# A planned attention and feed-forward kernel: other durations for GpSimd and SP, and a delay before GpSimd may take a high part

## The chip, the cores and the metric

The kernel runs on one core of a Trainium2 chip. The core has five engines that run side by side, each through its own list of instructions in a fixed order: TensorE (PE, matrix products), VectorE (DVE), ScalarE (ACT), GpSimd (POOL) and SyncE (SP), which here only issues transfers (DMA). An instruction waits until the instructions on other engines whose results it needs have signalled. The metric is the device time of one execution in microseconds (us); a smaller time is better.

## The reference

Two stages, the output of the first being the input of the second. Inputs are float32: q, k, v of 8 batches, 8 heads, 576 positions, 64 columns; f of 8 x 8 x 576; w_in of 512 x 2048 and w_out of 2048 x 512.

```python
scores = scale * np.matmul(q, k.transpose(0, 1, 3, 2))
log_f = np.log(np.clip(f, 0.0001, 1.0))
cum = np.cumsum(log_f, axis=-1)
decay = cum[:, :, :, None] - cum[:, :, None, :]
scores = np.where(causal, -1000000000.0, scores + decay)
scores = scores - np.max(scores, axis=-1, keepdims=True)
attn = np.exp(scores)
attn = attn / (np.sum(attn, axis=-1, keepdims=True) + 1e-09)
attn_out = np.matmul(attn, v)
...
x = attn_out.transpose(0, 2, 1, 3).reshape(4608, 512)
h = x @ w_in
g = np.where(h >= 1, h, np.where(h <= -1, 0.0, (h + 1) ** 2 / 4))
return g @ w_out
```

So: causal attention with a decay that depends on the distance of two running sums, and then for each of 4608 tokens a feed-forward layer with a piecewise quadratic activation between two products.

## The kernel before

**Split numbers.** Most products run on float16 pairs: a float32 value, scaled by a power of two, is written as a high part (the value rounded to float16) and a low part (value minus high part, again float16). A product of two such values takes three products of halves. The high part is a multiplication by a scale, which ScalarE, VectorE or GpSimd can do (helper `times`, L395 to L401: ScalarE at L397, GpSimd at L401); the low part is a two-input instruction on VectorE, and it waits for the high part.

**Attention** (`attention`, L687 on) runs in 36 jobs, one for two heads of one batch, with batch 0 cut in two (`CUTS`). A job loads q and k (L717, L721) and the running sums, spread over all partitions (tile ck, L730), all issued by SP. From job 12 on, ScalarE finds the largest magnitudes (L780), a small exchange through TensorE spreads them (`across`, L440 on), GpSimd makes the factors (`factors`, L795), q and k are split (tile qs; high parts by `X`, low parts at L818 and L824), and SP issues one DMA transpose of the 20 blocks (L833) and two copies that swap halves (tile qkT, L837). The first jobs work in float32 through TensorE transposes (L756, L767, L1021).

For each of the five row tiles r of 128 queries (the last has 64 for each head, both heads in one tile), GpSimd makes the decay into a tile sd or sdr: a multiply-add over (r + 1) x 128 columns (L934), then a select that puts a very small number above the diagonal (L938). TensorE makes the scores into one of three banks (tile s; L846). VectorE adds both and takes the row minimum (its sign is turned; L971), which also empties the bank; ScalarE takes the exponential and its row sum (L980); GpSimd or VectorE adds the small constant (`inverse`, L986), VectorE takes the reciprocal (L992). Then the weights are scaled and split into tile pr: the high part on ScalarE or GpSimd (by `X`), the low part on VectorE (L1056). SP issues the DMA transpose of pr into pT (L1068; for the last row tile two, L1073). TensorE multiplies pT with the split v (tile vs, L896), and ScalarE and VectorE write the two halves of x (L912, L913).

**Feed-forward** (`moe`, L1098 on) runs over 18 chunks of 256 tokens, and for each over 8 blocks of 256 columns of w_in: 24 matmuls into ph (L1119); ScalarE makes the scaled rectified value (L1128) and its square (L1131), VectorE joins them into u (L1132, which empties ph), then come the high part of g (`X`; L397 or L401), the low part of g on VectorE (L1138), and 12 matmuls into po (L1146), 8 that need only the high part and 4 that need the low one. At the chunk's end po goes to ot and out to memory. The weights are loaded at the start in eight blocks and split there (`weight_split`): the high part on ScalarE, the low part (`low`) in two GpSimd instructions (L572, L573) or in one of VectorE.

**The order** is not written by hand. Every instruction group is registered by `Order.op` with its engine, an estimated duration, what it reads and writes, and a priority; an operation may name other engines with their durations (`other`) and, for each, a time `late` that must have passed since the operation became ready. `Order.plan` then plays the whole kernel through with these durations: whenever an engine is free it takes, in order of priority, the first operation that is ready and whose buffers are free. Engines are asked in the order of their first registered operation, and the first one registered is a memset on GpSimd. What is played through becomes the order in which each engine's instructions are written, and also settles which engine does an operation that several can do. At run time nothing is changed any more: an instruction whose inputs come later than planned holds up all that stands behind it on its engine.

The helpers give the durations: `act_us`, `dve_us`, `pool_us` by the number of columns; `V`, `A`, `G`, `M` register for VectorE, ScalarE, GpSimd and TensorE; `X` registers an operation with a choice of engines ("AG": ScalarE or GpSimd); `L` registers a transfer with the time SP needs to issue it and its size, `T` a DMA transpose with its number of blocks. After a GpSimd operation the plan lets GpSimd go on 0.04 us before its end (`OVER`). The plan lets a transfer land at the later of its issue's end plus a constant, and of the point at which the DMA engines have moved its bytes plus a constant. `hold` keeps job 9 and later from starting before a planned time, 27 us apart (`PACE`).

Of the kernel before, what the change touches and what calls it, by code (L numbers as in the profile page):

```python
# [37 lines left out]
WLOAD = (-98.0, -50.0, -40.0, -30.0, -6.0, 0.0, 6.0, 12.0)  # L38
SLACK = 0.3
WINDOW = 1000  # L40

# [30 lines left out]
class Order:  # L72
# [42 lines left out]
    def plan(self):  # L115
        ops = self.ops
        n = len(ops)
# [23 lines left out]
        while done < n:  # L141
# [5 lines left out]
            while again:  # L147
                again = False
                for eng, l in waiting.items():
# [57 lines left out]
                    if size:  # L207
                        kind = "DMA"
                        begin = max(t, dma - 4.0)
                        free[eng] = begin + dur  # L210
                        dma = max(dma, begin + 0.3) + size
                        end = max(begin + dur + 1.7, dma + 1.4)
                    else:
                        begin = t
                        if eng == "PE" and md != mode:
                            begin += 0.1
                            mode = md
                        end = begin + dur
                        free[eng] = end - self.OVER[eng]
# [41 lines left out]
def pool_us(n):  # L261
    return 0.36 + 0.001 * n

# [6 lines left out]
def kernel(  # L270
# [149 lines left out]
    def T(blocks, emit, reads=(), writes=(), prio=0.0):  # L420
        op("SP", 0.95 + 0.055 * blocks + (2.3 if blocks > 20 else 0.0), emit, reads, writes, prio, blocks * 0.0328 * 6.0)

# [17 lines left out]
    def across(m, n, mkeys, prio):  # L440
# [16 lines left out]

        op("POOL", 0.55, make, ["ident"], [top, dg], prio, other=[("DVE", 0.4, 0.0)])
        M(
# [18 lines left out]
    def decay_sums():  # L478
# [3 lines left out]
        pr = -99.0  # L482
        L(0.5, 0.15, lambda: nc.sync.dma_start(fl[0:nb, 0:S], f.rearrange("b h s -> (b h) s")), [], key, pr)
        V(S, lambda: nc.vector.tensor_scalar(
# [7 lines left out]
        ), ["flz"], key, pr, 1.35)  # L492
        L(0.5, 0.15, lambda: nc.sync.dma_start(cum_d, cum), key, ["cum_d"], pr)
        pt = Buf(f_pool)
# [17 lines left out]
    def weight_load(i, prio):  # L512
# [4 lines left out]
        for j in range(2):  # L517
            src, raw = srcs[j], raws[RAW[i][j]]
            n = src.shape[1] // 2
            for part in range(2):  # L520
                dst = raw[:, 2 * DM * part:2 * DM * (part + 1)].rearrange("p (t c) -> p t c", t=n)
                L(
                    0.45, 0.524, lambda dst=dst, src=src, part=part, n=n: nc.sync.dma_start(
                        dst, src[:, n * part:n * part + n, :]
                    ), [], [rawkeys[RAW[i][j]][part]], prio + 0.1 * j + 0.05 * part,
                )

    def weight_split(i, prio):
# [29 lines left out]
        for j in range(2):  # L558
# [15 lines left out]

            op("POOL", 3.5, low, [("sw", i)], key + [("pl", i, j)], prio, other=[("DVE", 1.46, 0.0)])

    def load_values(b, hp, prio):
        s_ = v[b, 2 * hp:2 * hp + 2]
        t = vres[hp]
        for hh in range(2):  # L580
            L(0.45, 0.131, lambda hh=hh: nc.sync.dma_start(
                t[:, hh, 0:LAST, :], s_[hh, 0:FULL, :].rearrange("(t p) d -> p t d", p=P)
            ), [], [("v", hp, hh)], prio)
        L(0.45, 0.033, lambda: nc.sync.dma_start(
            t[0:64, :, LAST, :], s_[:, FULL:S, :].rearrange("h p d -> p h d")
# [56 lines left out]
    def moe_scales(b, k, first, last, prio):  # L642
# [37 lines left out]

        G(1.2, make, [("sv", b), ("rv", b), ("lim", k)] + need, [z.key], prio)
        return z
# [4 lines left out]
    def attention(ji):  # L687
# [11 lines left out]
        for j, src in enumerate((q, k)):  # L699
# [16 lines left out]
            for hh in range(2):  # L716
                L(0.45, 0.131, lambda part=part, s_=s_, hh=hh, full=full, t0=t0: nc.sync.dma_start(  # L717
                    part()[1][:, hh, 0:full - t0, :], s_[hh, P * t0:P * full, :].rearrange("(t p) d -> p t d", p=P)
                ), [], [keys[hh]], pr - 20)
            if r1 == NT5:  # L720
                L(0.45, 0.033, lambda part=part, s_=s_, nt=nt: nc.sync.dma_start(  # L721
                    part()[1][0:64, :, nt - 1, :], s_[:, FULL:S, :].rearrange("h p d -> p h d")
# [4 lines left out]
        for h in range(2):  # L727
            ck = Buf(ck_first if p < NPE else ck_pool)
            cks.append(ck)
            L(0.5, 0.29, lambda ck=ck, h=h: nc.sync.dma_start(  # L730
                ck.ap[:, 0:s1], cum_d[bh + h:bh + h + 1, 0:s1].broadcast_to([P, s1])
# [39 lines left out]
        else:  # L771
# [24 lines left out]

            G(0.9, factors, [mk, sc, "cq"], [sg, cs], pq)
            nsig, nalpha = (lambda: sg.ap[:, 0:1]), (lambda: sg.ap[:, 1:2])
# [37 lines left out]
            for h in range(2):  # L836
                L(0.5, 0.3, lambda h=h: nc.sync.dma_start(  # L837
                    qt.ap[64 * h:64 * h + 64, n:n + nqe], qt.ap[64 - 64 * h:128 - 64 * h, 0:nqe]
# [80 lines left out]
        for r in range(r0, r1):  # L919
# [5 lines left out]
            for h in range(2):  # L925
# [16 lines left out]

                G(pool_us(wid) + 0.34, decay, [cks[h], "sdz"] + sigkey, [(sd, h if r == LAST else 0)], pw)

# [45 lines left out]

            op("POOL", 0.26, inverse, [(sm, i) for i in range(nh)], [rc], pw, other=[("DVE", 0.22, 0.0)])
            V(0, lambda rc=rc, nh=nh: nc.vector.reciprocal(rc.ap[:, 0:nh], rc.ap[:, 0:nh]), [], [rc], pw, 0.25)  # L992
            part = int(r >= 2)
# [46 lines left out]
            else:  # L1040
# [5 lines left out]
                for i, sd in enumerate(sds):  # L1046
# [3 lines left out]
                    def rows_(sd=sd, cols=cols):  # L1050
# [3 lines left out]
                        e, prv()[:, :, 0, i, :], rows_(), rc.ap[:, i:i + 1]  # L1054
                    ), kk + [rc], [(prb, i)], pw + 0.5)
                    V(cols, lambda i=i, prv=prv, rows_=rows_, rc=rc: nc.vector.scalar_tensor_tensor(  # L1056
# [41 lines left out]
    def moe(ch, first, last, z, prio):  # L1098
# [10 lines left out]
        for fb in range(first, last + 1):  # L1109
# [3 lines left out]
            for fi in range(2):  # L1113
# [22 lines left out]
                e, g.ap[:, 0], u.ap, z.r[:, i:i + 1]  # L1136
            ), [u, z.key], [(g, 0)], pf - 1e4)
            V(512, lambda i=i, u=u, g=g: nc.vector.scalar_tensor_tensor(  # L1138
# [101 lines left out]
```

## Time and profile before

| | |
|---|---|
| median of 3 runs | 1122.61 us |
| lowest, highest | 1117.22, 1122.67 us |
| the profiled execution | 1119.65 us |
| its span, first to last instruction | 1117.9 us |
| mean granted clock of TensorE | 0.985 |

Transfers of the page that belong to what SP issues (operation, count, size, median us from issue to landing):

```profile
ck<-cum_d SPq DMA_DIRECT2D x62, 288.0 KB, 3.9
...
qkT<-qkT SPq DMA_DIRECT2D x48, 160.0 KB, 3.5
```

In the profile, PE is TensorE's products and PEld its weight loads, DVE is VectorE, ACT ScalarE, POOL GpSimd, SP SyncE. A group's row names the line, the engine, the operation, what is written and read, its shape and count, then the total busy time in us and the mean of one in ns, then the idle time of the engine just before these instructions and who ended it. A row of the waits reads "who waited <- who ended the wait: us in total, how many, the longest". A row of busy time over a stretch gives for each engine the busy us and the number of instructions, then the granted clock of TensorE, the DMA engines' share and GB/s. The lines themselves stand in the prediction.

### The profile page before, as it was taken

How to read it: one execution, taken by the hardware profiler on the slowest of the kernel's cores; microseconds unless marked ns; L12 is line 12 of the kernel's file. 1: busy time of each engine (PE TensorE's matmuls, PEld its weight loads, DVE VectorE, ACT ScalarE, POOL GpSimd, SP SyncE). 2: the span in 40 equal slices, each digit the busy share in tenths (PEclk: the TensorE clock that was granted, in tenths of full speed). 3: DMA queues.
4: the chain of work that ended last, by engine and by line, in shares of the span. 5: the costliest groups of instructions: out<-in, count | busy, mean ns of one | idle time of the engine just before them, and what ended most of it. 6: DMA issues, size and time to landing. Idle time of an engine off the chain costs nothing. (4 is left out here: it accounts for less than half of the span.)

```text
span 1117.9 us, 24870 instructions
## 1 busy us (share of the span) xinstructions
PE 1047.2 (94%) x8805; PEld 696.7 (62%) x8805; DVE 815.0 (73%) x2033; ACT 651.2 (58%) x1396; POOL 673.5 (60%) x1153
## 2 busy tenths in 40 slices
PE   4878999899999999999999999999999999999998
PEld 2545655556755766666766665665766677677665
DVE  5878888887888978888887878887877864232332
ACT  3556766665766765676757675766657653232232
POOL 2578787776777766876776776776676741111110
PEclk9879999999999999999999999999999999999999
DMA  7845455776987878789878886887768662000000
GB/s 190 294 128 162 135 139 106 137 144 139 169 168 156 170 145 166 152 152 167 154 149 156 156 173 144 161 169 141 149 141 167 116 105 37 21 20 20 1 19 20
DMA packets 390620, 146.37 MB, mean 131 GB/s; under 512 B 367328, under 2 KB 368352, under 8 KB 390496
## 3 DMA queue, kind: packets, MB, share of 16 engines
q1 hardware_dynamic: 385312, 135.35, 60.0%
q10 hardware_dynamic: 5184, 9.44, 2.5%
q8 instruction: 69, 1.13, 0.4%
q14 instruction: 55, 0.45, 0.2%
HBM read 65.68 MB, written 9.58 MB: 67 GB/s over the span
## 5 line engine op out<-in xcount | busy, mean ns | idle before, releaser
L1146 PE MATMUL po<-place,g 128*128 128x512 f16 x1728 | 405.4, 381 | 10.9 <-POOL g L401 8.2
L1119 PE MATMUL ph<-x,place 128*128 128x256 f16 (+3 forms) x4608 | 407.0, 247 | 3.0 <-DVE u L1132 1.5
L1119 PEld LDWEIGHTS <-place 128*128 128x128 f16 x4608 | 355.7, 98 | 57.2 <-issue 7.4
L1146 PEld LDWEIGHTS <-g 128*128 128x128 f16 x1728 | 162.5, 98 | 199.1 <-POOL g L401 14.3
L1128 ACT ACTIVATE u<-ph,z 128x512 f32<-128x512 f32 x144 | 110.9, 771 | 173.1 <-PE ph L1119 153.3
L401 POOL TENSOR_SCALAR g<-u,z 128x512 f16<-128x512 f32 x94 | 74.4, 791 | 218.7 <-DVE u L1132 203.7
L1132 DVE SCALAR_TENSOR_TENSOR u<-ph,z,u 128x512 f32<-128x512 f32 x144 | 107.4, 747 | 122.9 <-ACT u L1131 121.9
L980 ACT ACTIVATE sdr<-sdr,nm 128x512 f32<-128x512 f32 (+3 forms) x246 | 135.9, 553 | 82.3 <-DVE nm L971 75.0
L934 POOL TENSOR_SCALAR sdr<-ck,sg,cqs 128x128 f32<-128x128 f32 (+1 forms) x192 | 157.5, 820 | 34.2 <-DVE pr L1056 26.7
L1138 DVE SCALAR_TENSOR_TENSOR g<-u,z,g 128x512 f16<-128x512 f32 x144 | 113.6, 790 | 57.4 <-POOL g L401 48.3
L1056 DVE SCALAR_TENSOR_TENSOR pr<-sdr,nm,pr 128x128 f16<-128x128 f32 (+1 forms) x224 | 130.6, 614 | 5.9 <-POOL pr L401 3.1
L971 DVE CUSTOM_DVE_ANT_0 sdr<-s,sdr,sg 128x128 f32<-128x128 f32 (+1 forms) x192 | 100.9, 542 | 15.3 <-PE s L846 12.1
L938 POOL TENSOR_SCALAR_AFFINE_SELECT sdr<-sdr 128x128 f32<-128x128 f32 x246 | 95.9, 390 | 18.1
L846 PE MATMUL s<-qkT 128*128 128x128 f16 (+5 forms) x576 | 94.6, 297 | 9.8 <-DVE nm L971 7.0
L397 ACT ACTIVATE pr<-sdr,nm 128x256 f16<-128x256 f32 (+3 forms) x133 | 70.2, 549 | 48.9 <-issue 18.5
L1131 ACT ACTIVATE u<-u 128x512 f32<-128x512 f32 x144 | 90.6, 630 | 4.5
L896 PE MATMUL s<-pT,vs 128*64 128x320 f16 (+4 forms) x1176 | 68.9, 263 | 5.8 <-DVE nm L971 2.5
L896 PEld LDWEIGHTS <-vs 128*64 128x64 f16 x1176 | 56.5, 110 | 28.2 <-issue 19.2
L401 POOL TENSOR_SCALAR pr<-sdr,nm 128x512 f16<-128x512 f32 (+3 forms) x91 | 54.5, 601 | 17.3 <-DVE nm L992 12.9
L846 PEld LDWEIGHTS <-qkT 128*128 128x128 f16 (+1 forms) x576 | 41.5, 101 | 37.2 <-issue 19.9
L934 POOL TENSOR_SCALAR sd<-ck,sg,cqs 64x576 f32<-64x576 f32 x48 | 42.3, 881 | 20.6 <-DVE pr L1056 18.5
L767 PE MATMUL s<-qkT 64*128 64x128 f32 (+5 forms) x192 | 49.2, 513 | 5.4 <-DVE nm L971 4.3
(147 smaller groups left out, 1215.9 us busy)
## 6 DMA issues: line engine op xcount, KB each, us to landing
ck<-cum_d SPq DMA_DIRECT2D x62, 288.0 KB, 3.9
out_dram<-ot ACTq DMA_DIRECT2D x36, 256.0 KB, 3.0
v<-in_v_dram SPq DMA_DIRECT2D x64, 128.0 KB, 3.3
qk<-in_k_dram SPq DMA_DIRECT2D x64, 128.0 KB, 2.7
qkT<-qkT SPq DMA_DIRECT2D x48, 160.0 KB, 3.5
qk<-in_q_dram SPq DMA_DIRECT2D x56, 128.0 KB, 3.2
place<-in_moe_w_in_dram SPq DMA_DIRECT2D x10, 512.0 KB, 6.2
place<-in_moe_w_out_dram SPq DMA_DIRECT2D x8, 512.0 KB, 8.5
```

The costliest lines, as they stand in the source:

```text
L401: nc.gpsimd.tensor_scalar(out=out, in0=in_, scalar1=scale, scalar2=0.0, op0=ALU.mult, op1=ALU.add)
L846: nc.tensor.matmul(sp[p0:p1, 0:c1 - c0], lhsT=tq[:, h, q0 - s0:q0 - s0 + p1 - p0], rhs=tk[:, h, c0:c1], start=(c == 0), stop=(c == 1),)
L896: nc.tensor.matmul(av.ap[64 * h:64 * h + 64, c0:n], lhsT=vs.ap[:, vl, h, t, :], rhs=pT.ap[:, t, pl, h, c0:n], start=(t == 0 and pi == 0), ...
L934: nc.gpsimd.tensor_scalar(out=sd.ap[p0:p1, 0:wid], in0=cks[h].ap[p0:p1, 0:wid], scalar1=ns if p < NQK else ns[p0:p1], scalar2=cqs()[p0:p1, ...
L971: V(0, lambda o=i + ci, sd=sd, sp=sp[ci], c0=c0, c1=c1, nm=nm: nc.vector.tensor_tensor_reduce(out=sd.ap[:, c0:c1], in0=sp.ap[:, 0:c1 - c0] ...
L980: A(wid, lambda i=i, sd=sd, wid=wid, nm=nm, sm=sm: nc.scalar.activation(sd.ap[:, 0:wid], sd.ap[:, 0:wid], AF.Exp, bias=nm.ap[:, i:i + 1], ...
L1056: V(cols, lambda i=i, prv=prv, rows_=rows_, rc=rc: nc.vector.scalar_tensor_tensor(out=prv()[:, :, 1, i, :], in0=rows_(), scalar=rc.ap[:, i ...
L1119: nc.tensor.matmul(ph.ap[:, fi * TC + a0:fi * TC + a1], lhsT=wi[fb][:, wl, t, fi * P:(fi + 1) * P], rhs=xs[b][:, t, xl, s0:s0 + a1 - a0], ...
L1128: A(512, lambda i=i, ph=ph, u=u: nc.scalar.activation(u.ap, ph.ap, AF.Relu, scale=z.u[:, i:i + 1], bias=z.h[:, i:i + 1]), [ph, z.key], [u] ...
L1132: V(512, lambda i=i, ph=ph, u=u: nc.vector.scalar_tensor_tensor(out=u.ap, in0=ph.ap, scalar=z.t[:, i:i + 1], in1=u.ap, op0=ALU.max, op1=AL ...
L1138: V(512, lambda i=i, u=u, g=g: nc.vector.scalar_tensor_tensor(out=g.ap[:, 1], in0=u.ap, scalar=z.r[:, i:i + 1], in1=g.ap[:, 0], op0=ALU.mu ...
L1146: nc.tensor.matmul(po.ap[i], lhsT=g.ap[:, gl, fi * TC + i * P:fi * TC + (i + 1) * P], rhs=wo[fb][:, wl, fi, :], start=(fb == first and fi ...
```

## The change

Three things change, all of them in the numbers that the planner is given; the instructions themselves stay the same, as does what they compute.

- The planned durations of what GpSimd does: `pool_us` (high parts), the decay pair, the low part of the weights, the scales and factors, the small exchanges and `inverse`.
- The planned durations of what SP issues: loads and copies (`L`), and the DMA transposes, by a new function `turn_us` of the number of blocks; and the constants for the landing of any transfer (1.7 to 2.0 and 1.4 to 1.6 us).
- `LATE`: GpSimd may be given the high part of g only 0.6 us after it became ready, and the high part of pr only 0.4 us after. Before, both were 0: GpSimd could be given them at once.

```diff
+LATE = (0.6, 0.4)
...
-                        end = max(begin + dur + 1.7, dma + 1.4)
+                        end = max(begin + dur + 2.0, dma + 1.6)
...
-    return 0.36 + 0.001 * n
+    return 0.3 + 0.00095 * n
+
+
+def turn_us(blocks):
+    return 1.2 + max(0, blocks - 8) * 0.08 + max(0, blocks - 12) * 0.12
...
-        op("SP", 0.95 + 0.055 * blocks + (2.3 if blocks > 20 else 0.0), emit, reads, writes, prio, blocks * 0.0328 * 6.0)
+        op("SP", turn_us(blocks), emit, reads, writes, prio, blocks * 0.0328 * 6.0)
...
-        op("POOL", 0.55, make, ["ident"], [top, dg], prio, other=[("DVE", 0.4, 0.0)])
+        op("POOL", 0.7, make, ["ident"], [top, dg], prio, other=[("DVE", 0.4, 0.0)])
...
-        L(0.5, 0.15, lambda: nc.sync.dma_start(fl[0:nb, 0:S], f.rearrange("b h s -> (b h) s")), [], key, pr)
+        L(0.55, 0.15, lambda: nc.sync.dma_start(fl[0:nb, 0:S], f.rearrange("b h s -> (b h) s")), [], key, pr)
...
-        L(0.5, 0.15, lambda: nc.sync.dma_start(cum_d, cum), key, ["cum_d"], pr)
+        L(0.55, 0.15, lambda: nc.sync.dma_start(cum_d, cum), key, ["cum_d"], pr)
...
-                    0.45, 0.524, lambda dst=dst, src=src, part=part, n=n: nc.sync.dma_start(
+                    0.47, 0.524, lambda dst=dst, src=src, part=part, n=n: nc.sync.dma_start(
...
-            op("POOL", 3.5, low, [("sw", i)], key + [("pl", i, j)], prio, other=[("DVE", 1.46, 0.0)])
+            op("POOL", 4.35, low, [("sw", i)], key + [("pl", i, j)], prio, other=[("DVE", 1.46, 0.0)])
...
-            L(0.45, 0.131, lambda hh=hh: nc.sync.dma_start(
+            L(0.54, 0.131, lambda hh=hh: nc.sync.dma_start(
...
-        L(0.45, 0.033, lambda: nc.sync.dma_start(
+        L(0.65, 0.033, lambda: nc.sync.dma_start(
...
-        G(1.2, make, [("sv", b), ("rv", b), ("lim", k)] + need, [z.key], prio)
+        G(1.8, make, [("sv", b), ("rv", b), ("lim", k)] + need, [z.key], prio)
...
-                L(0.45, 0.131, lambda part=part, s_=s_, hh=hh, full=full, t0=t0: nc.sync.dma_start(
+                L(0.54, 0.131, lambda part=part, s_=s_, hh=hh, full=full, t0=t0: nc.sync.dma_start(
...
-                L(0.45, 0.033, lambda part=part, s_=s_, nt=nt: nc.sync.dma_start(
+                L(0.65, 0.033, lambda part=part, s_=s_, nt=nt: nc.sync.dma_start(
...
-            L(0.5, 0.29, lambda ck=ck, h=h: nc.sync.dma_start(
+            L(0.53, 0.29, lambda ck=ck, h=h: nc.sync.dma_start(
...
-            G(0.9, factors, [mk, sc, "cq"], [sg, cs], pq)
+            G(1.3, factors, [mk, sc, "cq"], [sg, cs], pq)
...
-                L(0.5, 0.3, lambda h=h: nc.sync.dma_start(
+                L(0.62, 0.3, lambda h=h: nc.sync.dma_start(
...
-                G(pool_us(wid) + 0.34, decay, [cks[h], "sdz"] + sigkey, [(sd, h if r == LAST else 0)], pw)
+                G(1.08 + 0.0006 * wid if r < LAST else 1.25, decay, [cks[h], "sdz"] + sigkey, [(sd, h if r == LAST else 0)], pw)
...
-            op("POOL", 0.26, inverse, [(sm, i) for i in range(nh)], [rc], pw, other=[("DVE", 0.22, 0.0)])
-            V(0, lambda rc=rc, nh=nh: nc.vector.reciprocal(rc.ap[:, 0:nh], rc.ap[:, 0:nh]), [], [rc], pw, 0.25)
+            op("POOL", 0.31, inverse, [(sm, i) for i in range(nh)], [rc], pw, other=[("DVE", 0.22, 0.0)])
+            V(0, lambda rc=rc, nh=nh: nc.vector.reciprocal(rc.ap[:, 0:nh], rc.ap[:, 0:nh]), [], [rc], pw, 0.24)
...
-                    ), kk + [rc], [(prb, i)], pw + 0.5)
+                    ), kk + [rc], [(prb, i)], pw + 0.5, late=LATE[1])
...
-            ), [u, z.key], [(g, 0)], pf - 1e4)
+            ), [u, z.key], [(g, 0)], pf - 1e4, late=LATE[0])
```

The first two changes with X are the high part of pr (`late=LATE[1]`) and that of g (`late=LATE[0]`); the only use of `turn_us` is in `T`.

## The prediction

> **What bounds the kernel now.** I read the page first: the span, the engines' busy time, the slices.
>
> ```profile
> span 1117.9 us, 24870 instructions
> PE 1047.2 (94%) x8805; PEld 696.7 (62%) x8805; DVE 815.0 (73%) x2033; ACT 651.2 (58%) x1396; POOL 673.5 (60%) x1153
> ...
> PE   4878999899999999999999999999999999999998
> ...
> PEclk9879999999999999999999999999999999999999
> ```
>
> TensorE works for 94% of the span, and from the slices the missing 6% is mostly at the left edge. The order of instructions on each engine is fixed when the kernel is built, so TensorE's idle time is time in which the next instruction in its written order was not ready. The next view is the busy time in three stretches: start, middle, tail.
>
> ```profile
> core 0: us, PE busy (x) PEld busy (x) DVE busy (x) ACT busy (x) POOL busy (x), PEclk, DMA share, GB/s
> 0.00:200.00 200.00, 163.47 (x908) 100.96 (x909) 160.78 (x397) 116.63 (x249) 135.28 (x216) 0.91 0.58 164
> 200.00:930.00 730.00, 700.87 (x6386) 470.06 (x6386) 597.65 (x1561) 481.37 (x1072) 513.86 (x903) 1.00 0.79 152
> 930.00:1118.00 188.00, 182.88 (x1515) 125.72 (x1512) 56.54 (x76) 53.16 (x76) 24.35 (x35) 1.00 0.05 16
> ```
>
> The subtraction gives TensorE's idle time: 200 - 163.47 = 36.5 us at the start, 730 - 700.87 = 29.1 in the middle, 188 - 182.88 = 5.1 in the tail. In the tail, with attention over, TensorE works 183 of 188 us on feed-forward blocks. So the end moves by what changes in TensorE's idle time (and slow clock) before it, and by nothing else: another engine that finishes earlier gives nothing that TensorE doesn't notice. In the middle VectorE is busy 598 / 730 = 82%, GpSimd 70%, ScalarE 66%: none is the bound, each can be late at a place. Which places, says the list of waits of TensorE in the middle:
>
> ```profile
> PE s L846 <- DVE nm L971: 7.0, 12, 0.9
> PE po L1146 <- POOL g L401: 4.9, 7, 1.2
> ...
> PE s L896 <- DVE nm L971: 2.5, 4, 0.9
> PE po L1146 <- ACT g L397: 2.3, 6, 0.6
> PE s L846 <- DMA qkT<-qkT: 2.2, 3, 0.9
> PE s L896 <- DMA pT<-pr: 2.1, 2, 1.3
> ```
>
> Columns: total us, times, longest. Three families carry 21.0 of the 29.1 us: the high part of g (4.9 + 2.3 = 7.2), score banks that VectorE has not yet emptied (7.0 + 2.5 = 9.5), transposes and copies issued by SP (2.2 + 2.1 = 4.3). The start has the same kinds and one wait that nothing here touches, the first load:
>
> ```profile
> PE ph L756 <- DMA qk<-in_q_dram: 12.0, 1, 12.0
> PE s L767 <- DVE nm L971: 4.3, 7, 1.3
> ...
> PE po L1146 <- POOL g L401: 2.7, 3, 1.4
> ```
>
> **The change part by part.** No instruction is added or removed. The planner gets other durations, so it writes another order, and it may give a multiplication to another engine. What this is worth is the lateness that the old order had not planned.
>
> *High parts (LATE).* The planner asks engines in the order of their first operation; the first one planned is a memset on GpSimd, so GpSimd is asked before ScalarE and takes a high part of g or of pr whenever it is free. After the change it may take one only 0.6 us (g) or 0.4 us (pr) after it became ready. The busy time of the instructions on g, first GpSimd's, then ScalarE's:
>
> ```profile
> 200.00:930.00 730.00, 44.56 (x54) 1.00 0.79 152
> 930.00:1118.00 188.00, 24.35 (x35) 1.00 0.05 16
> ```
>
> ```profile
> 200.00:930.00 730.00, 33.14 (x46) 1.00 0.79 152
> ```
>
> A ScalarE instruction of the middle lasts 481.37 / 1072 = 0.45 us on average, and g has the highest priority, so in 0.6 us ScalarE is nearly always free once: I estimate that about 90 of the 100 g of the middle, and all 35 of the tail, go to ScalarE. The durations, and those of the low part that waits behind:
>
> ```profile
> L401 POOL TENSOR_SCALAR g<-u,z x94: 690/695/1707, 70.0 to 1109.9; 128x512 f16<-128x512 f32 x94
> ```
>
> ```profile
> L397 ACT ACTIVATE g<-u,z x50: 704/722/725, 73.9 to 898.6; 128x512 f16<-128x512 f32 x50
> ```
>
> ```profile
> L1138 DVE SCALAR_TENSOR_TENSOR g<-u,z,g x144: 730/751/1278, 71.2 to 1110.7; 128x512 f16<-128x512 f32 x144
> ```
>
> (min/median/max in ns.) On ScalarE a g is 0.72 us every time. On GpSimd it is 24.35 / 35 = 0.70 in the tail, where little runs beside it, 44.56 / 54 = 0.83 in the middle, and up to 1.71. The planner had 0.36 + 0.512 - 0.04 = 0.83, so g itself was planned right on the mean; the single late one was not. The move of some 44 g costs ScalarE 44 x 0.72 = 32 us; of pr, whose groups are
>
> ```profile
> L397 ACT ACTIVATE pr<-sdr,nm 128x256 f16<-128x256 f32 (+3 forms) x133 | 70.2, 549 | 48.9 <-issue 18.5 <-ACT sdr L980 15.7 <-DVE nm L992 10.5
> ...
> L401 POOL TENSOR_SCALAR pr<-sdr,nm 128x512 f16<-128x512 f32 (+3 forms) x91 | 54.5, 601 | 17.3 <-DVE nm L992 12.9
> ```
>
> I let two thirds of the 91 move, 60 x 0.55 = 33 us. ScalarE then has 481 + 32 + 33 = 546 of 730 us, 75%; still less than VectorE, so it lies beside other work. It is not free: the exponentials and the first pass over ph queue behind each moved part, up to 0.72 us, and a late ph pass makes the next g late. What comes of it on TensorE is bounded by the waits on g: at best all 7.2 us go. At worst the ten that still go to GpSimd start 0.6 us later and the 90 on ScalarE are each late as often as its 46 were (2.3 us in 46, so 4.5 in 90): 4.5 + 10 x 0.6 = 10.5, that is 3.3 more than now. ScalarE's own row is the nearest: 4.5 us, and of ten late ones most are covered, since only 13 of 100 g were waited for. That is 2.7 less than 7.2. The start's 2.7 us on GpSimd's g shrink likewise; as its order is open, I count 0.8 of them: **-3.5** together.
>
> *GpSimd's durations.* The groups by shape for the decay pairs and for the low part of a weight block:
>
> ```profile
> L938 POOL TENSOR_SCALAR_AFFINE_SELECT sdr<-sdr 128x128 f32<-128x128 f32 x246 | 95.9, 390 | 18.1
> ...
> L934 POOL TENSOR_SCALAR sdr<-ck,sg,cqs 128x512 f32<-128x512 f32 x48 | 46.4, 967 | 5.1 <-DVE pr L1056 5.1
> ...
> L934 POOL TENSOR_SCALAR sdr<-ck,sg,cqs 128x128 f32<-128x128 f32 x48 | 36.5, 760 | 12.8 <-DVE pr L1056 6.4 <-DMA ck<-cum_d 4.9 <-POOL vs L401 0.6
> ...
> L573 POOL TENSOR_TENSOR place<-place,place 128x1024 f16<-128x1024 f32 x4 | 11.9, 2966 | 0.3
> ...
> L572 POOL TENSOR_SCALAR place<-place,sw 128x1024 f32<-128x1024 f32 x4 | 5.2, 1300 | 3.7 <-ACT place L564 3.6
> ```
>
> A pair of width 128 takes 0.760 + 0.390 = 1.15 us; planned were 0.36 + 0.128 + 0.34 - 0.04 = 0.79, now 1.12. At width 512 it is 1.36; planned 1.17, now 1.35. So GpSimd ran 0.2 to 0.4 us late per pair, and the plan caught up only where GpSimd idles. Late decays hold up VectorE's combination, which holds the score banks: that is the 9.5 us of the middle and 4.3 of the start. All 13.8 gone is one end. But VectorE, 82% busy, is itself the releaser there, and its durations are not changed; the other end is that the new order adds as many such waits as the row at L896 holds, +2.5. The releaser being VectorE, I stay near nothing: **-2**.
>
> *SP's durations.* The instructions of the transposes:
>
> ```profile
> L833 SPq DMA_TRANSPOSE qkT<-qs x24: 3023/3366/3792, 249.4 to 892.5; - x24
> ```
>
> ```profile
> L1068 SPq DMA_TRANSPOSE pT<-pr x112: 1188/1394/3399, 158.3 to 924.2; - x112
> ```
>
> The transpose of q and k (20 blocks) was planned 0.95 + 1.1 = 2.05 us and takes 3.37; now 1.2 + 0.96 + 0.96 = 3.12. It delays everything behind it on SP's queue: the two copies qkT<-qkT, loads of ck, the next pT. With the later landings too (+0.2 to 0.3 us) the products are placed later, behind feed-forward work. One end: all 4.3 us of DMA waits go; the other, nothing, because the products stand later and the score banks fill in a bunch. Only five waits make up the 4.3, so this is a handful of places: **-1.5**.
>
> *Start.* The low part planned 3.5 us takes 1.30 + 2.97 = 4.27, now 4.35. The order of the weight blocks, transposes and early jobs is dealt anew. Idle there besides the first load is 36.5 - 12.0 = 24.5 us; what one stretch is worth, good or bad, shows here:
>
> ```profile
> 105.00:110.00 5.00, 2.01 (x9) 1.78 (x9) 3.51 (x6) 0.99 (x3) 4.43 (x8) 0.74 0.98 274
> 110.00:115.00 5.00, 5.00 (x23) 2.85 (x23) 3.64 (x10) 2.71 (x6) 4.47 (x7) 0.57 0.16 36
> ```
>
> TensorE stands for 5 - 2.01 = 3.0 us, then has a granted clock of 0.57 for 5 us: 3.0 + 0.26 x 2.01 + 0.43 x 5 = 5.7 us for one gap. One gap less is -5.7, one or two more +5.7 to +11.4; I take **0** and keep the ends.
>
> *Tail.* g moves to ScalarE at equal duration, and the low part starts behind it as before; TensorE has no idle there but the last wait. In the timeline of the last two blocks
>
> ```profile
> 1107.31 0.70 POOL L401 TENSOR_SCALAR g<-u,z 128x512 f16<-128x512 f32 x1 [7.11 <-DVE u L1132]
> 1107.54 0.78 ACT L1128 ACTIVATE u<-ph,z 128x512 f32<-128x512 f32 x1 [1.18 <-PE ph L1119]
> ```
>
> ScalarE's next pass would start behind g, at about 1107.9 instead of 1107.54: +0.4 us at most on the last block, **0** taken; the cover is the back products of the block before it.
>
> **The sum.** -3.5 - 2 - 1.5 + 0 + 0 = -7.0 us of TensorE idle. The profiled execution took 1119.65 us, its span of 1117.9 and 1.75 around it; so 1112.65. The median of the three runs is 1122.61, 2.96 above the profiled one (runs from 1117.22 to 1122.67); I keep to the profiled execution. Faster or slower means by over 0.5%, 5.6 us, about what a measurement of this kernel can tell from no change.
>
> **The rivals.**
>
> *The order is only dealt anew.* The planner's error is not its mean but the spread (GpSimd's g from 0.69 to 1.71 us), and a new order meets as many late inputs at other places. For it: the waits are many and small, 34 of them make 21.0 us, none over 1.3. Against: they concentrate on operations whose duration the planner had wrong by known amounts. Idle time stays: 1119 us. Chance 0.18.
>
> *GpSimd's time is not its own.* While VectorE runs its two-input passes (L1138, L1056), GpSimd's instructions stretch, so a planned constant is right only where the neighbours are as in the trace before. Moved off GpSimd, the g are stretched no more (0.83 to 0.72), but the decays move against other VectorE passes and their traced means no longer hold. Then the term of GpSimd's durations and that of SP behind it vanish, and half of the first stays: 1119.65 - 1.8 = 1118, no difference. For it: the 1707 ns and VectorE's own 1278 against 751. Against: the median of g is 695, near the minimum, so most are not hit. Chance 0.12. The Trainium skill, "SBUF — State Buffer", section "SBUF: two separate sides", states the rule behind it: GpSimd and a VectorE instruction with two SBUF inputs contend for one port pair, an exclusive lock held for the whole instruction, and the loser fully blocks. By that rule, the maximum of 1707 ns is one g behind one VectorE pass, and the trace agrees in size (0.69 + 0.75 = 1.44, with part of another).
>
> *A new gap at the start, slower.* One mechanism: with the low parts of the weights planned 0.85 us longer on GpSimd, six of them on the way to the first feed-forward blocks, TensorE's order at 50 to 150 us puts a block in front that is not ready, TensorE stands for 3 us or more, and the granted clock falls as at 105 to 115 us. It decides from the point where a gap is so long that the clock falls: 5.7 us for one gap. With the three gains failing, one or two gaps give 1119.65 + 5.7 to 11.4, I say 1127. For it: the start has several such gaps already (the slices 7 and 8 of TensorE, the clock's 8 and 7). Against: a planner with truer durations should place blocks later, not earlier. Chance 0.20. The Trainium skill, "TensorE: Matmul & The Clock Gate", section "Part 1: The HAM clock gate (the "warmup" mystery)", says that the clock halves after an idle window of about 3.4 us and comes back after as long of work; by that rule a gap shorter than the window would cost only itself, and the row's 0.57 behind 3.0 us of idle fits a half-rate with a recovery.
>
> **How the numbers follow.** Forecast, faster: 0.50 (1101 to 1114). Order only dealt anew 0.18 and GpSimd's stretch 0.12, both within 0.5%: 0.30. Slower: 0.20. The range reaches down to all of the first and third terms with one gap less (7.2 + 4.3 + 5.7 = 17.2 and a little of the second: 1101) and up to the slower case: 1127.
>
> **What would show it.** Right: in the middle GpSimd holds some 10 g and ScalarE 90, ScalarE near 75% and GpSimd near 60% (514 - 44 x 0.83 - 60 x 0.60 = 441 of 730); TensorE's waits on g fall from 7.2 to about 4, those on nm from 9.5 to 7.5, those on SP's transfers below 3; idle in the middle near 22 us. Wrong: the waits on g move to ScalarE's row at the same sum; new rows for ScalarE (u, x, the exponentials) in TensorE's or VectorE's waits; the start's idle over 42 us or a lower clock there than 0.91. The forecast fails if idle in the middle stays near 29, or if the start changes by more than the middle.

## The result, and the profile after

The changed kernel takes 1104.60 us (median of 4 runs, 1103.03 to 1105.94); the kernel before, in 4 runs, 1120.18 us. The ratio is 0.9861, with a 95% interval from 0.9826 to 0.9897: 1.4% faster. The profiled execution took 1103.03 us, against 1119.65 before.

Five lines are new above the functions, so every line from `pool_us` on stands up to five further down: L846 is now L851, L896 is L901, L971 is L976, L397 is L402, L401 is L406.

The page of the changed kernel, first its span and busy times, then two of the slices:

```profile
span 1101.2 us, 24739 instructions
...
PE 1046.9 (95%) x8805; PEld 699.9 (64%) x8805; DVE 804.5 (73%) x2029; ACT 719.4 (65%) x1518; POOL 586.0 (53%) x1034
...
PE   4879999999999999999999999999999999999998
...
PEclk9689989999999999999999999999999999999999
```

TensorE's busy time is the same as before (1046.9 and 1047.2 us), and the span is shorter by 16.7 us. So it is idle time that went: 1117.9 - 1047.2 = 70.7 us before, 1101.2 - 1046.9 = 54.3 now, 16.4 less. Where it went, the busy times of the three stretches show (the last one reaches 0.8 us past the span's end):

```profile
0.00:200.00 200.00, 165.08 (x947) 102.17 (x948) 169.35 (x418) 129.07 (x276) 132.29 (x215) 0.90 0.63 170
200.00:930.00 730.00, 715.60 (x6530) 483.90 (x6529) 583.46 (x1544) 520.59 (x1142) 453.71 (x820) 1.00 0.81 150
930.00:1102.00 172.00, 166.26 (x1333) 113.78 (x1330) 51.68 (x69) 69.77 (x101) 0.00 (x0) 0.99 0.05 16
```

Idle time of TensorE: start 34.9 us (36.5 before), middle 14.4 (29.1), tail 4.9 within the span (5.0). The middle gave 14.7 of the 16.4. Its matmul count rose from 6386 to 6530: what was squeezed out of the gaps is feed-forward work that is missing from the tail. The waits of TensorE in that middle stretch:

```profile
PE s L901 <- DVE nm L976: 4.5, 9, 1.0
PE s L851 <- DVE nm L976: 1.6, 7, 0.3
...
PE po L1151 <- ACT g L402: 1.2, 4, 0.4
...
PE s L851 <- DMA qkT<-qkT: 0.7, 1, 0.7
```

All three families of the prediction shrank: high parts of g from 7.2 to 1.2 us, score banks from 9.5 to 6.1, SP's transfers from 4.3 to 0.7 (the row of pT<-pr is gone). That is 13.0 of the 14.7 us. The start, by its list of waits, kept its kinds of waits:

```profile
PE s L772 <- DVE nm L976: 5.7, 7, 2.1
...
PE po L1151 <- ACT g L402: 1.6, 2, 1.4
```

Who makes the high parts: the busy time of the instructions on g in the middle, first GpSimd's, then ScalarE's; in the tail GpSimd has none.

```profile
200.00:930.00 730.00, 3.88 (x5) 1.00 0.81 150
```

```profile
200.00:930.00 730.00, 70.22 (x98) 1.00 0.81 150
```

ScalarE now makes 98 g of the middle (46 before), GpSimd 5 (54 before). ScalarE is busy for 521 of 730 us there (71%), GpSimd for 454 (62%).

### The profile page after: what moved, and what is told of

Its sections match the earlier page's. It is cut to its first block, busy times and chain, and to the rows that moved or that the text cites. A ratio compares the mean times of both kernels' runs of the same rounds, so it can differ in the third digit from the quotient of the medians.

```text
span 1101.2 us, 24739 instructions
## 1 busy us (share of the span) xinstructions
PE 1046.9 (95%) x8805; PEld 699.9 (64%) x8805; DVE 804.5 (73%) x2029; ACT 719.4 (65%) x1518; POOL 586.0 (53%) x1034
## 3 DMA queue, kind: packets, MB, share of 16 engines
q8 instruction: 69, 1.13, 0.4%
## 5 line engine op out<-in xcount | busy, mean ns | idle before, releaser
L939 POOL TENSOR_SCALAR sdr<-ck,sg,cqs 128x128 f32<-128x128 f32 (+1 forms) x192 | 161.1, 839 | 57.7 <-DVE pr L1061 44.8
L1143 DVE SCALAR_TENSOR_TENSOR g<-u,z,g 128x512 f16<-128x512 f32 x144 | 115.9, 805 | 47.0 <-ACT g L402 44.9
L402 ACT ACTIVATE g<-u,z 128x512 f16<-128x512 f32 x139 | 99.8, 718 | 57.3 <-DVE u L1137 55.9
L1061 DVE SCALAR_TENSOR_TENSOR pr<-sdr,nm,pr 128x128 f16<-128x128 f32 (+1 forms) x224 | 125.4, 591 | 9.6 <-ACT pr L402 8.0
L976 DVE CUSTOM_DVE_ANT_0 sdr<-s,sdr,sg 128x128 f32<-128x128 f32 (+1 forms) x192 | 100.3, 542 | 20.3 <-PE s L851 15.4
L943 POOL TENSOR_SCALAR_AFFINE_SELECT sdr<-sdr 128x128 f32<-128x128 f32 x246 | 100.5, 408 | 18.1
L402 ACT ACTIVATE pr<-sdr,nm 128x384 f16<-128x384 f32 (+3 forms) x153 | 80.3, 551 | 37.3 <-issue 12.9
L851 PE MATMUL s<-qkT 128*128 128x128 f16 (+5 forms) x576 | 91.5, 298 | 3.8 <-DVE nm L976 1.6
L901 PEld LDWEIGHTS <-vs 128*64 128x64 f16 x1176 | 57.5, 110 | 28.3 <-issue 20.1
L901 PE MATMUL s<-pT,vs 128*64 128x320 f16 (+4 forms) x1176 | 67.9, 263 | 6.9 <-DVE nm L976 4.5
L991 POOL TENSOR_SCALAR nm<-nm 128x2 f32<-128x2 f32 (+1 forms) x77 | 19.1, 248 | 84.0 <-ACT sdr L985 66.9
L851 PEld LDWEIGHTS <-qkT 128*128 128x128 f16 (+1 forms) x576 | 41.7, 101 | 31.6 <-issue 15.0
L406 POOL TENSOR_SCALAR pr<-sdr,nm 128x512 f16<-128x512 f32 (+3 forms) x71 | 42.0, 594 | 30.8 <-DVE nm L997 27.0
```

The source lines that it names most:

```text
L402: nc.scalar.activation(out, in_, AF.Copy, scale=scale)
L851: nc.tensor.matmul(sp[p0:p1, 0:c1 - c0], lhsT=tq[:, h, q0 - s0:q0 - s0 + p1 - p0], rhs=tk[:, h, c0:c1], start=(c == 0), stop=(c == 1),)
L901: nc.tensor.matmul(av.ap[64 * h:64 * h + 64, c0:n], lhsT=vs.ap[:, vl, h, t, :], rhs=pT.ap[:, t, pl, h, c0:n], start=(t == 0 and pi == 0), ...
L939: nc.gpsimd.tensor_scalar(out=sd.ap[p0:p1, 0:wid], in0=cks[h].ap[p0:p1, 0:wid], scalar1=ns if p < NQK else ns[p0:p1], scalar2=cqs()[p0:p1, ...
L943: nc.gpsimd.affine_select(sd.ap[p0:p1, q0:wid], sd.ap[p0:p1, q0:wid], pattern=[[-1, wid - q0]], channel_multiplier=1, base=0, compare_op=A ...
```

## The experiments

Twelve kernels. The table shows for each the ratio to the kernel before with its 95% interval, and from its profile, for 200 to 930 us: TensorE's idle time and its waits on the three families (us). "g" adds the rows of po behind g, from GpSimd and from ScalarE; "score banks" adds the rows of L846 and L896 (L851 and L901) behind nm; "SP" adds those of qkT<-qkT and pT<-pr. The letters of theories and rivals are those of the expectations.

| kernel | ratio | interval | idle | g | SP | score banks |
|---|---|---|---|---|---|---|
| before | 1 | | 29.1 | 7.2 | 4.3 | 9.5 |
| changed | 0.9861 | 0.9826 to 0.9897 | 14.4 | 1.2 | 0.7 | 6.1 |
| late_only | 0.9940 | 0.9920 to 0.9960 | 22.4 | 4.4 | 1.7 | 10.7 |
| durations_only | 0.9859 | 0.9841 to 0.9877 | 18.0 | 0.9 | 2.6 | 5.7 |
| pool_only | 0.9951 | 0.9932 to 0.9969 | 25.0 | 0.9 | 4.7 | 10.1 |
| sp_only | 0.9985 | 0.9968 to 1.0001 | 23.8 | 6.9 | 0.7 | 5.8 |
| before_redealt | 0.9967 | 0.9955 to 0.9980 | 28.5 | 5.1 | 4.2 | 9.0 |
| after_redealt | 0.9820 | 0.9806 to 0.9835 | 12.8 | 0.7 | 1.2 | 4.1 |
| decay_only | 0.9965 | 0.9953 to 0.9977 | 23.9 | 1.3 | 4.3 | 8.7 |
| decay_over | 0.9809 | 0.9795 to 0.9824 | 14.7 | 3.5 | 1.5 | 6.7 |
| before_margin | 0.9992 | 0.9975 to 1.0009 | 27.7 | 3.8 | 1.9 | 10.0 |
| no_decay | 0.9967 | 0.9952 to 0.9981 | 27.6 | 3.5 | 0.6 | 16.9 |
| late_over | 0.9748 | 0.9733 to 0.9762 | 10.6 | 0.8 | 0.0 | 5.3 |
| late_over2 | 0.9751 | 0.9728 to 0.9773 | 12.8 | 0.4 | 4.6 | 5.1 |

### The parts alone

**late_only** is the changed kernel with every duration put back:

```diff
-                        end = max(begin + dur + 2.0, dma + 1.6)
+                        end = max(begin + dur + 1.7, dma + 1.4)
...
-    return 0.3 + 0.00095 * n
+    return 0.36 + 0.001 * n
...
-    return 1.2 + max(0, blocks - 8) * 0.08 + max(0, blocks - 12) * 0.12
+    return 0.95 + 0.055 * blocks
...
-                G(1.08 + 0.0006 * wid if r < LAST else 1.25, decay, [cks[h], "sdz"] + sigkey, [(sd, h if r == LAST else 0)], pw)
+                G(pool_us(wid) + 0.34, decay, [cks[h], "sdz"] + sigkey, [(sd, h if r == LAST else 0)], pw)
```

> The delay for GpSimd's high parts with all durations of the kernel before. Theory A (each cause of lateness gives its own share): the waits of TensorE on g in the middle (7.2 us before) fall below 2, those on nm (9.5) and on SP's transfers (4.3) stay; 1113 to 1116 us. Rival B (the move of high parts off GpSimd is the whole of it): all of the gain, 1103 to 1107 us. Rival C (the new order is luck): anything from 1105 to 1130, with no tie between what was changed and which waits fall.

1114.02 us. Its waits of TensorE in the middle:

```profile
PE s L851 <- DVE nm L976: 7.6, 14, 1.1
PE po L1151 <- ACT g L402: 4.4, 7, 1.4
PE s L901 <- DVE nm L976: 3.1, 7, 0.7
```

GpSimd no longer holds up a g, but ScalarE does, for 4.4 us: more than the 2 us that was expected. The delay by itself moves the high parts; it doesn't make them punctual. The time lies in theory A's range; of its waits, those on SP's transfers were to stay at 4.3 and are 1.7, though SP's durations are the old ones. Rival B falls: the move off GpSimd is not the whole.

**durations_only** is the opposite, all new durations and `LATE` at zero:

```diff
-LATE = (0.6, 0.4)
+LATE = (0.0, 0.0)
```

> All new durations, GpSimd may take a high part at once as before. Theory A: waits on nm and on SP's transfers fall as in the changed kernel (to about 6 and 1 us), waits on g fall partly because the plan now knows GpSimd's backlog (to about 4); 1108 to 1112 us. Rival B: no gain, 1117 to 1122 us. Rival C: anything.

1105.23 us: the whole gain in time, and more than expected. TensorE's waits in the middle on what the delay was to help:

```profile
PE po L1151 <- ACT g L402: 0.5, 1, 0.5
PE po L1151 <- POOL g L406: 0.4, 1, 0.4
```

GpSimd still makes 43 g of the middle here, 36.28 us by the busy time of that tile, and nearly all are in time: 0.9 us of waits on g against 7.2. So GpSimd is not too slow for g as such. What made g late before, the trace of the kernel before tells in part. TensorE waited seven times for a g of GpSimd in the middle, 4.9 us together; four of these waits, 3.7 us, are of this kind:

```profile
419.63 0.74 DVE L1132 SCALAR_TENSOR_TENSOR u<-ph,z,u 128x512 f32<-128x512 f32 x1
420.29 1.40 DVE L1056 SCALAR_TENSOR_TENSOR pr<-sdr,nm,pr 128x512 f16<-128x512 f32 x2
420.46 1.71 POOL L401 TENSOR_SCALAR g<-u,z 128x512 f16<-128x512 f32 x1 [1.29 <-DVE u L1132]
...
422.23 2.76 PE L1146 MATMUL po<-place,g 128*128 128x512 f16 x12 [1.01 <-POOL g L401]
```

Nothing stood ahead of this g: GpSimd had been idle for 1.29 us and began 0.09 us after u was done. The g itself was long, 1.71 us beside two low parts of pr on VectorE, where most take 0.69. Two of the other three (1.0 us) had decays ahead of them on GpSimd between the end of u and the start of g. That part follows the planned duration: in the five orders with the old one for the decay pair and no delay it is 0.6 to 2.9 us (2.9 in sp_only); in durations_only, pool_only and decay_only there is none, though decay_over has one wait of 1.0 us. Long g, however, are as frequent with the new durations: 10 of 43 over 1 us in durations_only, 10 of 54 before. In durations_only just one wait, of 0.4 us, stands behind them. Why the new order covers them isn't shown.

**pool_only** and **sp_only** split the durations, both with `LATE` at zero. The first is durations_only with what belongs to SP put back (issue times, landing constants, `turn_us`), the second is durations_only with what belongs to GpSimd put back (`pool_us`, the decay pair, `low`, `factors`, `make`, `inverse`, and the 0.01 us of VectorE's reciprocal).

> GpSimd's new durations alone. Theory A: waits on nm and on g fall by a third to a half, those on SP's transfers stay at 4.3; 1111 to 1116 us. Rival B: 1117 to 1122 us.

> SP's new durations and landing times alone. Theory A: TensorE's waits on SP's transfers fall from 4.3 to below 1.5 us, the rest stays; 1115 to 1119 us. Rival B: 1117 to 1122 us.

1115.96 and 1118.38 us. The waits of pool_only, in the middle:

```profile
PE s L851 <- DVE nm L976: 8.1, 16, 1.5
PE s L851 <- DMA qkT<-qkT: 4.4, 7, 1.1
...
PE po L1151 <- ACT g L402: 0.9, 3, 0.4
```

and of sp_only:

```profile
PE po L1151 <- POOL g L406: 6.2, 9, 1.3
...
PE po L1151 <- ACT g L402: 0.7, 2, 0.4
...
PE s L851 <- DMA qkT<-qkT: 0.3, 1, 0.3
```

With GpSimd's durations g falls from 7.2 to 0.9 us while the waits on SP's transfers are 4.7; with SP's durations the transfers fall to 0.7 while g stays at 6.9. The score banks came out against both expectations: pool_only was to lower them by a third to a half and has 10.1 us, sp_only was to leave them and has 5.8. In time the two bring 0.5% and 0.15% (for sp_only the interval includes no change), together 1.4%. In idle time they nearly add up: span less busy time is 70.7 us before, 1114.9 - 1046.7 = 68.2 in pool_only, 1116.4 - 1052.1 = 64.3 in sp_only and 1103.1 - 1043.2 = 59.9 in durations_only, so 2.5 and 6.4 us less apart and 10.8 together. What doesn't add up is TensorE's busy time: 0.5 us less, 4.9 more, and 4.0 less together (see the last section).

### How much is the draw of an order

**before_redealt** and **after_redealt** change a number of the plan that has nothing to do with the change, so that all orders are dealt anew:

```diff
-SLACK = 0.3
+SLACK = 0.31
```

> The kernel before with the plan's margin SLACK at 0.31 instead of 0.30 us: another order, no duration nearer to the trace. Theory A: within 4 us of the kernel before, and the waits on g and on SP's transfers stay near 7 and 4 us in the middle. Rival C (orders scatter, the change drew a good one): it may lie 10 us or more off on either side.

> The changed kernel with SLACK at 0.31: another order with the new durations. Theory A: within 4 us of the changed kernel's 1104.6, and waits on g below 2 us, on SP's transfers below 2. Rival C: it loses a good part of the gain, 1110 to 1120 us.

1116.81 us, 0.33% under the kernel before measured beside it; 1100.17 us, against the changed kernel's 1104.60. A mere re-deal therefore moved either kernel by about 4 us, in one try for each. The gain of 1.4% is three to four times that, and the after_redealt order keeps it (1.8%), so rival C, luck, does not carry it. But differences of 0.15 to 0.5% (pool_only, sp_only, decay_only) are hardly larger than a re-deal, and the waits of one family scatter too. Among the three orders that have all old durations and no delay (before, before_redealt and before_margin below), g has 7.2, 5.1 and 3.8 us and SP's transfers 4.3, 4.2 and 1.9. Over all kernels the tie is clear for g: 3.5 to 7.2 us in the six with the old duration of the decay pair, 0.4 to 1.3 in seven of the eight with a longer one (3.5 in decay_over). For the score banks there is no such line: 5.8 to 16.9 and 4.1 to 10.1.

### Which duration

**decay_only** takes the kernel before and changes the decay pair alone; **no_decay** is durations_only with the decay pair alone put back (0.7 + 0.001 per column is the old sum):

```diff
-                G(pool_us(wid) + 0.34, decay, [cks[h], "sdz"] + sigkey, [(sd, h if r == LAST else 0)], pw)
+                G(1.08 + 0.0006 * wid if r < LAST else 1.25, decay, [cks[h], "sdz"] + sigkey, [(sd, h if r == LAST else 0)], pw)
```

```diff
-                G(1.08 + 0.0006 * wid if r < LAST else 1.25, decay, [cks[h], "sdz"] + sigkey, [(sd, h if r == LAST else 0)], pw)
+                G(0.7 + 0.001 * wid, decay, [cks[h], "sdz"] + sigkey, [(sd, h if r == LAST else 0)], pw)
```

> The kernel before with the planned duration of the decay pair alone changed (0.8 to 1.2 us becomes 1.16 to 1.39). Theory A: this is GpSimd's largest error (320 pairs, 0.2 to 0.4 us each), so it does what all of GpSimd's durations did: 1114 to 1118 us, waits on g below 2.5 us. Rival C: no tie; the waits on g may stay at 7.

> All new durations but that of the decay pair, which is planned as before (0.2 to 0.4 us too short); no delay. If the decay pair is the part that makes the durations work together: 1113 to 1119 us and waits on g back to 5 us or more. If SP's and the other durations do it: 1104 to 1110 us.

decay_only takes 1115.75 us, no_decay 1116.82. TensorE's waits in the middle, decay_only first (its line numbers are those of the kernel before):

```profile
PE s L846 <- DMA qkT<-qkT: 4.3, 4, 3.1
...
PE po L1146 <- ACT g L397: 1.0, 2, 0.6
...
PE po L1146 <- POOL g L401: 0.3, 1, 0.3
```

```profile
PE s L851 <- DVE nm L976: 10.7, 18, 1.3
PE s L901 <- DVE nm L976: 6.2, 8, 2.1
...
PE po L1151 <- POOL g L406: 2.7, 7, 0.9
```

The decay pair alone brings g to 1.3 us and leaves SP's 4.3. Without it, with everything else new, the gain is 0.3%: the score banks are waited for 16.9 us, g for 3.5 (5 or more had been expected). From no_decay to durations_only, one duration, lies 1.1%, about three times a re-deal, and the largest difference in the waits is at the score banks (16.9 against 5.7). The gain rests on this part, though by itself it brings no more than a re-deal.

### Truth or margin

**decay_over** is durations_only with the decay pair planned 0.36 us longer than in the trace, an error as large as the old one, to the other side:

```diff
-                G(1.08 + 0.0006 * wid if r < LAST else 1.25, decay, [cks[h], "sdz"] + sigkey, [(sd, h if r == LAST else 0)], pw)
+                G(1.44 + 0.0006 * wid if r < LAST else 1.61, decay, [cks[h], "sdz"] + sigkey, [(sd, h if r == LAST else 0)], pw)
```

> All new durations, no delay, but the decay pair planned another 0.36 us longer than traced, so the plan errs as much as before, to the other side. If truth matters (theory A): the plan leaves gaps that the chip doesn't need and places work late; 1110 to 1118 us, and TensorE waits for other things than g. If only margin matters (the plan must not promise GpSimd's results too early): as with the new durations, 1103 to 1108 us.

1099.07 us, below both ranges. It is not slower than durations_only; its interval ends below that of durations_only (0.9824 against 0.9841), by little more than a re-deal would explain. Theory A in the form "the nearer to the truth, the better" falls: promising GpSimd's decays too early costs (no_decay), promising them 0.36 us too late didn't.

**before_margin** asks whether any margin would do; it is the kernel before with the margin for TensorE's inputs doubled:

```diff
-SLACK = 0.3
+SLACK = 0.6
```

> The kernel before, all its old durations, with SLACK at 0.6 instead of 0.3 us: TensorE's work is planned only 0.6 us after its inputs. Theory D (what helps is margin against late inputs, wherever it is put): a good part of the gain, 1103 to 1112 us, waits of TensorE down across all families. Theory A (each duration has to be near its truth): little, 1114 to 1120 us, since SP's and GpSimd's queues still run late by more than 0.3 us.

1120.28 us, no change (0.9975 to 1.0009), although the waits on g fell to 3.8 us and those on SP's transfers to 1.9. Margin for all of TensorE's inputs is not it.

**late_over** and **late_over2** are the changed kernel, delay included, with the decay pair 0.36 and 0.72 us longer than traced:

```diff
-                G(1.08 + 0.0006 * wid if r < LAST else 1.25, decay, [cks[h], "sdz"] + sigkey, [(sd, h if r == LAST else 0)], pw)
+                G(1.44 + 0.0006 * wid if r < LAST else 1.61, decay, [cks[h], "sdz"] + sigkey, [(sd, h if r == LAST else 0)], pw)
```

(in late_over2 1.8 and 1.97 in place of 1.44 and 1.61.)

> The changed kernel, delay included, with the decay pair planned another 0.36 us longer. If the delay and the durations cure the same waits (high parts that come late from a GpSimd with a backlog), nothing is left for the delay to add: 1096 to 1101 us, as with the longer decay alone (1099.1). If they are separate, 1090 to 1095 us.

> As late_over (1091.0 us), with the decay pair planned 0.72 us longer than traced instead of 0.36. If more margin on GpSimd's decays goes on helping (theory D, on GpSimd alone): 1085 to 1090 us. If 0.36 us already covers the spread and more only leaves planned gaps: 1091 to 1098 us, the idle time of TensorE in the middle above late_over's 10.6 us. If late_over is a lucky order among those that scatter by 4 us: 1096 to 1103 us.

1091.03 and 1093.87 us; by the ratios, 0.9748 and 0.9751, the two are equal, and 2.5% faster than the kernel before: the best of the study. late_over in the middle, by the busy times of its engines:

```profile
200.00:930.00 730.00, 719.38 (x6586) 488.19 (x6586) 593.50 (x1588) 542.55 (x1183) 424.20 (x778) 1.00 0.80 152
```

TensorE is idle for 10.6 us there. The delay added nothing to the time on top of the traced durations (0.9861 against 0.9859; 5.6 us less idle over the span, 3.7 us more busy time). On top of the longer ones it goes with 0.6% (0.9809 to 0.9748), about one and a half re-deals, and with waits on g of 0.8 instead of 3.5 us: the time is the one expected if the delay does something of its own, but at that size a re-deal isn't excluded. From the changed kernel to late_over lie 1.1%, three re-deals. Beyond 0.36 us nothing more comes. In late_over2, idle is 12.8 us and the waits on SP are back:

```profile
PE s L851 <- DMA qkT<-qkT: 2.4, 4, 1.2
PE s L901 <- DMA pT<-pr: 2.2, 3, 1.2
```

Why the longer duration helps is not settled. It gives margin to the decays, but it also makes GpSimd look fuller, so that the plan sends work elsewhere: GpSimd's busy time in the middle falls from 453.71 us in the changed kernel to 424.20 in late_over. The traced durations did the same without any delay: 513.86 us before, 479.63 in durations_only. No run separates the two.

## Why the prediction was right, and where not

It said 1112.65 us, faster, by less idle time of TensorE in the middle. The direction held, and so did the place: TensorE's idle time in the middle, in the three families that were named; 1104.60 lies in its range. The size was more than twice the forecast: idle time fell by 16.4 us, not 7.0. And the share of the parts did not hold: half of the forecast was to come from the delay, and the durations alone bring the whole gain in time. That the forecast came out in spite of this is in part luck.

- **What bounds.** Right: the span fell by 16.7 us, TensorE's idle time by 16.4.
- **High parts, -3.5.** This is the term that was mis-sized most, and it was tied to the wrong part of the change. In the middle the waits on g fell by 6.0 us, at the start from 2.7 to 1.6. That single long g were the trouble fits the trace before (3.7 of the 4.9 us behind g of 1.26 to 1.71 us). That the delay would cure it does not: the waits on g go without the delay (durations_only 0.9 us) and with the decay pair's duration alone (1.3 us), and with the delay alone 4.4 stay, within the 3.8 to 7.2 of the orders with nothing new. The prediction had worked out the error of the decay pair, but let it act on the score banks only. That duration cures the queue ahead of g, 1.0 us of the 4.9 before; why the waits behind long g go with it is open.
- **What moves.** Some 90 g to ScalarE: 98. Of the 91 instructions for pr, sixty were to move; the page of the changed kernel has

```profile
L402 ACT ACTIVATE pr<-sdr,nm 128x384 f16<-128x384 f32 (+3 forms) x153 | 80.3, 551 | 37.3 <-issue 12.9
...
L406 POOL TENSOR_SCALAR pr<-sdr,nm 128x512 f16<-128x512 f32 (+3 forms) x71 | 42.0, 594 | 30.8 <-DVE nm L997 27.0
```

  71 on GpSimd, so twenty moved. ScalarE came to 71%, not 75%, GpSimd to 62%, not 60%.
- **GpSimd's durations, -2.** The score banks went from 9.5 to 6.1 us in the middle and from 4.3 to 5.7 at the start, 2.0 less together. The number came out, but no run ties it to these durations alone: pool_only, which has them, shows 10.1 us in the middle, sp_only, which has not, 5.8, and the re-deal of the changed kernel 4.1. In that it is luck. That decays planned too short go with waits at the banks, once the rest is new, no_decay shows (16.9 against 5.7). The prediction's "0.2 to 0.4 us late per pair" holds for 128, 256 and 512 columns (0.36, 0.29, 0.19), but not for 384, by the kernel before with its shapes kept apart

```profile
L934 POOL TENSOR_SCALAR sdr<-ck,sg,cqs 128x384 f32<-128x384 f32 x48 | 35.3, 735 | 8.8 <-DVE pr L1056 8.1 <-DVE mk L424 0.5
```

  where 0.735 + 0.390 = 1.13 us stand against a planned 1.04: late by 0.08.
- **SP's durations, -1.5.** Mis-sized: 4.3 fell to 0.7, so -3.6. The end "all go" was nearer than the middle value taken. sp_only and no_decay, with SP's new durations, have 0.7 and 0.6 too. Part of it is the draw of an order: late_only has 1.7 us with SP's old durations, late_over2 4.6 with the new ones. That the terms add up was assumed as well; GpSimd's and SP's durations nearly add up in idle time (2.5 and 6.4 us apart, 10.8 together), but not in time, because busy time was taken as fixed.
- **Start 0, tail 0.** Right: idle 36.5 to 34.9 us and a granted clock of 0.91 and 0.90; 5.0 to 4.9 in the tail. (A g of 0.72 us from 1107.31 ends at 1108.0, not 1107.9; nothing hangs on it.)
- **Rival: the order is only dealt anew.** It is real, about 4 us in the one try for each kernel, and too small. The spread that it names is what most of the waits on GpSimd's g stood behind; with the durations alone 0.4 us of that is left, in decay_over 1.7.
- **Rival: GpSimd's time is not its own.** The effect is there: with the g gone, GpSimd's decays got a little slower, by the page of the kernel before and then of the changed one

```profile
L934 POOL TENSOR_SCALAR sdr<-ck,sg,cqs 128x128 f32<-128x128 f32 (+1 forms) x192 | 157.5, 820 | 34.2 <-DVE pr L1056 26.7
...
L938 POOL TENSOR_SCALAR_AFFINE_SELECT sdr<-sdr 128x128 f32<-128x128 f32 x246 | 95.9, 390 | 18.1
```

```profile
L939 POOL TENSOR_SCALAR sdr<-ck,sg,cqs 128x128 f32<-128x128 f32 (+1 forms) x192 | 161.1, 839 | 57.7 <-DVE pr L1061 44.8
...
L943 POOL TENSOR_SCALAR_AFFINE_SELECT sdr<-sdr 128x128 f32<-128x128 f32 x246 | 100.5, 408 | 18.1
```

  the multiply-add from 820 to 839 ns and the select from 390 to 408. Such 37 ns a pair are small beside the 80 to 360 that the plan had wrong, so on the mean the durations held, and the gain that the rival denied came. The Trainium skill, "SBUF — State Buffer", section "SBUF: two separate sides", lets the loser of the shared port pair wait for the whole instruction; this agrees with single g of 1.7 us beside two low parts of pr on VectorE, and says nothing of how often it happens (10 of the 54 g of the middle took over 1 us).
- **Rival: a new gap at the start.** It didn't come: idle and clock of the start are nearly those of before. The gap that the prediction priced lasted 3.1 us, from 104.9 to 108.0; the granted clock was 0.99 from 105 to 107.5 us and 0.50 from 107.5 to 112.5, so here the clock fell behind a gap shorter than the 3.4 us that the prediction cites.

## What to carry to other kernels

Where an order is fixed by a planner, compare its durations with the traced ones and begin with the operation that is planned too short and repeated most, on any engine. The wait can show elsewhere: another duration for the decays took the waits on g from 7.2 to 1.3 us. Before saying why an instruction is late, look at it in the trace, since it may have stood in a queue or have run long itself. Judge the corrections of several queues together: here two brought 0.5% and 0.15% apart and 1.4% together, though their idle time nearly added up. And measure what a mere re-deal of the order does, because parts below that size can't be told by time, and the waits of one family scatter by some us as well. In this kernel, decays planned too short cost time, and decays planned 0.36 us too long did not.

## What was not expected of the hardware

TensorE's busy time for the same 8805 matmuls is not a constant of the kernel. It was 1047.2 us before and 1046.9 after, but 1052.1 in sp_only and 1038.8 in late_over, by their pages:

```profile
PE 1052.1 (94%) x8805; PEld 700.9 (63%) x8805; DVE 811.9 (73%) x2024; ACT 649.7 (58%) x1393; POOL 672.8 (60%) x1165
```

```profile
PE 1038.8 (95%) x8805; PEld 697.2 (64%) x8805; DVE 809.4 (74%) x2070; ACT 730.9 (67%) x1538; POOL 548.6 (50%) x973
```

So sp_only's 6.4 us less of idle time (its span of 1116.4 less 1052.1 is 64.3, against 70.7) brought only 1.5 us of span, and late_over's 28.9 us of span (1117.9 to 1089.0) are 20.5 of idle and 8.4 of busy time. By lines, the feed-forward products take nearly the same in both (814.0 and 815.6 us); sp_only is longer in the score products (L851: 94.7 and 90.7; L772, in float32: 49.5 and 44.1) and in some small ones. What makes the same matmuls take less was not settled; it means that an account of idle time alone can be off by 5 to 10 us in this kernel (in late_over2 the busy time is 1036.7 us).
